# GroupNorm on one core: 16 instead of 12 chunks of each tile summed on TensorE, and SyncE's last wait moved from a branch to a semaphore increment

## The chip, the cores and the metric

The kernel runs on one core of a Trainium2 chip. The metric is the device time of one execution in microseconds (us). A kernel on one core has one number per execution.

Names: PE is TensorE, DVE is VectorE, ACT is ScalarE, POOL is GpSimd, SP is SyncE. A "q" behind a name (SPq) is that engine's queue of instructions that are not counted as work: waits, branches, DMA issues.

## The reference

```python
B, C, H, W = 128, 1024, 32, 16          # x is bfloat16; 32 groups of 32 channels
xr = x.reshape(B, 32, 32, H, W)
mu  = xr.mean(axis=(2, 3, 4), keepdims=True)
var = ((xr - mu) ** 2).mean(axis=(2, 3, 4), keepdims=True)
xn  = (xr - mu) / sqrt(var + 1e-5)
return xn.reshape(B, C, H, W) * g[None, :, None, None] + b[None, :, None, None]
```

Input and output are 134.2 MB each. A tile is 128 partitions (4 samples x 32 groups) of 16384 bfloat16 numbers, 4.19 MB; there are 32 tiles.

## The kernel before

Four engines work on a ring of six tiles in SBUF; POOL only makes constants at the start. For each tile:

- SP loads it, and later stores it from the same slot of the ring.
- The sum of each row is shared out. PE adds chunks of 512 columns into PSUM by multiplying them with an identity matrix. DVE adds the remaining columns pairwise in one instruction, whose accumulated result lands in PSUM beside PE's sums.
- ACT sums those 513 numbers to the mean, squares the tile around it in two halves, and makes the standard deviation.
- DVE makes scale and shift and normalises the tile in place with 32 instructions; it signals after each quarter.

The parts that matter, with cuts marked by `...`:

```python
SLOTS = 6                                   # ring of 6 tiles
RUNS = (2, 3, 3, 3, 3, 3, 3, 3, 3, 6)       # stores issued in a row, then the loads they free
NQ = 4
PE_CHUNKS = 12
MM_FREE = 512
PAIRED = F - PE_CHUNKS * MM_FREE            # columns paired on DVE; F = 16384

def on_sync(e):
    def load(j):
        if j >= SLOTS:
            e.wait_ge(st[j % SLOTS], 16 * (j // SLOTS))
        e.dma_start(out=slot(j), in_=x_v[j]).then_inc(ld[j % SLOTS], 16)
    def store(i):
        w = F // store_parts(i)             # the last tile goes in 4 parts, all others in 1
        for p in range(store_parts(i)):
            e.wait_ge(done, NQ * i + NQ // store_parts(i) * (p + 1))
            e.dma_start(out=..., in_=...).then_inc(...)
    ...
    e.wait_ge(s_fin, ...)                   # the last thing SP does

def one(c, t):                              # PE, per tile
    for k in range(PE_CHUNKS):
        if k == 0:                 e.wait_ge(ld[c], (t + 1) * 16)
        elif k == PE_CHUNKS - 2:   e.wait_ge(meaned[(c - 2) % SLOTS], t + 1)
        elif k == PE_CHUNKS - 1:   e.wait_ge(paired, t * SLOTS + (c + 1))
        mm = add_up(sums(c), slot(c)[:, k * MM_FREE : (k + 1) * MM_FREE], k)
    ...

def pair(i):                                # DVE, one tile ahead
    lo, n = PE_CHUNKS * MM_FREE, PAIRED // 2
    e.wait_ge(first_in, i + 1)
    e.scalar_tensor_tensor(out=jp[:], in0=part(i, lo, n), scalar=1.0, in1=part(i, lo + n, n),
        op0=ALU.mult, op1=ALU.add, accum_out=ps[...], saturate=False).then_inc(paired, 1)

with nc.Fori(0, NT, 1, engines=[e.engine]) as i:      # DVE's loop
    with e.If(i < NT - 1):
        e.drain()
        pair(i + 1)
    e.wait_ge(stded, i + 1)
    ...                                     # reciprocal, scale, shift: three short instructions
    for k, a in enumerate(parts):           # 32 normalising instructions
        ts = e.tensor_scalar(out=a, in0=a, scalar1=scl[:, k : k + 1], scalar2=bia[:, k : k + 1], ...)
        if (k + 1) % KQ == 0:
            ts.then_inc(done, 1)
```

## Time and profile before

| | before |
|---|---|
| median of 3 runs | 632.13 us (631.5 to 632.31) |
| span of the profiled run | 630.7 us |
| queue of loads and stores, share of 16 DMA engines | 99.1% |
| DVE busy | 529.6 us (84%) |
| ACT busy | 504.0 us (80%) |
| PE busy | 156.7 us (25%) |

First, lines of the profile's page of before. The first gives busy time and share of each engine; the rows under it cut the span into 40 equal slices: DMA is the busy share of the 16 DMA engines in tenths, GB/s what they moved. The last is the line of the queue with the loads and stores (packets, MB, share).

```profile
PE 156.7 (25%) x385; PEld 0.2 (0%) x2; DVE 529.6 (84%) x1185; ACT 504.0 (80%) x258; POOL 1.0 (0%) x8
...
DMA  8999999999999999999999999999999999999996
GB/s 366 432 432 409 434 436 432 432 434 434 428 432 432 432 434 430 434 430 432 432 432 428 432 432 432 432 432 432 432 432 432 432 426 432 430 430 436 432 421 271
...
q1 hardware_dynamic: 9648, 268.44, 99.1%
```

The GB/s row is flat, at 426 to 436 in nearly every slice, and the engines' rows are not. What sets the 432 GB/s, loads and stores together, is not shown. 268.4 MB at 432 GB/s are 621.4 us of the 630.7.

Second, the table by stretches for before: start and end, length, busy time and count of PE, PEld, DVE, ACT and POOL, the clock granted to PE, the DMA share, GB/s. The last two stretches are the end of the kernel.

```profile
75.00:200.00 125.00, 30.02 (x76) 0.00 (x0) 120.09 (x274) 114.28 (x58) 0.00 (x0) 0.60 1.01 434
200.00:400.00 200.00, 54.98 (x133) 0.00 (x0) 174.01 (x384) 164.96 (x85) 0.00 (x0) 0.59 1.00 432
400.00:540.00 140.00, 32.15 (x85) 0.00 (x0) 121.51 (x278) 115.66 (x59) 0.00 (x0) 0.59 1.00 432
613.00:620.00 7.00, 0.00 (x0) 0.00 (x0) 7.00 (x23) 0.00 (x0) 0.00 (x0) 0.50 0.89 375
624.00:629.00 5.00, 0.00 (x0) 0.00 (x0) 0.00 (x0) 0.00 (x0) 0.00 (x0) 0.50 0.23 98
```

Read the first row closely: from 75 to 200 us DVE is busy 120.09 of 125 us, 96%. The same row shows the DMA engines at a share of 1.01. (This view counts a packet, its time and its bytes, wholly in the stretch where it starts, so a share can come out a little over 1.)

Third, the timeline of before, only DVE's pairing instruction of four tiles: start, duration, engine, line, what it does, and in brackets how long DVE sat idle ahead of it and for whom.

```profile
203.16 5.49 DVE L254 SCALAR_TENSOR_TENSOR jp<-ring 128x5120 fp8e5 x1 [0.50 <-issue]
220.40 5.49 DVE L254 SCALAR_TENSOR_TENSOR jp<-ring 128x5120 fp8e5 x1 [0.50 <-issue]
237.63 5.49 DVE L254 SCALAR_TENSOR_TENSOR jp<-ring 128x5120 fp8e5 x1 [0.50 <-issue]
259.68 5.49 DVE L254 SCALAR_TENSOR_TENSOR jp<-ring 128x5120 fp8e5 x1 [5.30 <-PE ps L178]
```

Where a tile is already there, DVE needs 17.24 us from one pairing to the next. The DMA needs 8.39 MB (a load and a store) at 432 GB/s, 19.4 us. So every few tiles DVE runs out of tiles and waits, as at 259.68, for PE's first matmul of a tile, which itself waits for the load.

### The profile page before, as it was taken

Reading aid. Unit: us, or ns where it says so; the run is one execution under the profiler, and the core shown is the slowest. Engines: PE = TensorE matmul, PEld = TensorE weight load, DVE = VectorE, ACT = ScalarE, POOL = GpSimd, SP = SyncE. Lnnn points to the kernel's source line nnn. Section 1 sums busy time; section 2 is a strip of 40 time slices with the busy share of each in tenths; the row PEclk is TensorE's granted clock in tenths of the full one; section 3 lists DMA queues with packets and bytes.
Section 4 is the critical chain, followed back from the end, with each engine's and each line's share of the span. In section 5 each row is a group of like instructions: output and inputs, shape, how many; then the busy total and the mean of one; then the engine's idle time right before and its main releaser. Section 6 shows DMA issues by size and latency. Waiting matters only on the chain.

```text
span 630.7 us, 2595 instructions
## 1 busy us (share of the span) xinstructions
PE 156.7 (25%) x385; PEld 0.2 (0%) x2; DVE 529.6 (84%) x1185; ACT 504.0 (80%) x258; POOL 1.0 (0%) x8
## 2 busy tenths in 40 slices
PE   1433333212223220332053014202220430053000
PEld 0000000000000000000000000000000000000000
DVE  1669999999999999699789959995998699599963
ACT  0798999999999999689948977894999499859960
POOL 0000000000000000000000000000000000000000
PEclk9766655566665765666566557656665665565555
DMA  8999999999999999999999999999999999999996
GB/s 366 432 432 409 434 436 432 432 434 434 428 432 432 432 434 430 434 430 432 432 432 428 432 432 432 432 432 432 432 432 432 432 426 432 430 430 436 432 421 271
DMA packets 9745, 268.45 MB, mean 426 GB/s; under 512 B 1168, under 2 KB 1168, under 8 KB 1168
## 3 DMA queue, kind: packets, MB, share of 16 engines
q1 hardware_dynamic: 9648, 268.44, 99.1%
q10 hardware_dynamic: 96, 0.00, 0.0%
q14 instruction: 1, 0.01, 0.0%
HBM read 134.22 MB, written 134.22 MB: 426 GB/s over the span
## 4 chain that ended last, share of the span: by engine, by line
DMA 44%; ACT 40%; DVE 7%; issue 4%; PE 2%; DVEq 2%; SPq 0%
ACT ja L224 37%; DMA out_dram<-ring 28%; DMA ring<-in_x_dram 16%; DVE ring L287 6%; PE ps L178 2%; ACT jm L216 2%; DVEq L270 1%; ACT var L234 1%; ACT std L238 1%; DVE jp L254 1%; DVEq L273 0%; DVE bia L281 0%; DVE scl L277 0%; DVEq L275 0%; DVEq L254 0%
## 5 line engine op out<-in xcount | busy, mean ns | idle before, releaser
L224 ACT ACTIVATE ja<-ring,nm 128x8192 fp8e5<-128x8192 bf16 x64 | 455.8, 7122 | 2.1
L287 DVE TENSOR_SCALAR ring<-ring,scl,bia x1024 | 333.7, 413 | 1.2
L178 PE MATMUL ps<-ring,eye 128*128 128x512 bf16 x384 | 156.5, 581 | 424.9 <-DVE jp L254 292.5
L254 DVE SCALAR_TENSOR_TENSOR jp<-ring 128x5120 fp8e5 (+1 forms) x32 | 175.8, 5493 | 60.7 <-PE ps L178 48.7
L216 ACT ACTIVATE jm<-ps 128x513 fp8e5<-128x513 f32 x32 | 19.2, 602 | 98.7 <-PE ps L178 98.7
L275 DVE RECIPROCAL rstd<-std 128x1 f32 x32 | 6.3, 198 | 11.9 <-ACT std L238 11.9
L224 ACT ACTIVATION_READ_ACCUMULATOR ja<-ring,nm 128x1 f32 x64 | 11.9, 186 | 0.0
L281 DVE SCALAR_TENSOR_TENSOR bia<-scl,nm,gb 128x32 f32<-128x32 f32 x32 | 8.0, 251 | 4.2
L238 ACT ACTIVATE std<-sq,var 128x1 f32<-128x1 f32 x32 | 9.4, 294 | 1.0
L234 ACT ACTIVATE var<-sq,eps_t 128x1 f32<-128x1 f32 x32 | 9.4, 294 | 1.0
L266 DVE COPY gb<-gb_p 128x64 f32<-128x64 f32 x1 | 0.2, 225 | 11.5 <-PE gb_p L173 11.5
L277 DVE TENSOR_SCALAR scl<-gb,rstd 128x32 f32<-128x32 f32 x32 | 7.7, 241 | 1.1
L216 ACT ACTIVATION_READ_ACCUMULATOR jm<-ps 128x1 f32 x32 | 6.2, 194 | 0.0
L254 DVE DVE_READ_ACCUMULATOR jp<-ring (+1 forms) x32 | 4.5, 142 | 0.0
L173 PE MATMUL gb_p<-gb_b,rep 32*128 32x64 bf16 x1 | 0.2, 205 | 11.3 <-DMA gb_b<-in_b_dram 11.3
L212 ACT ACT_TABLE_LOAD x1 | 1.3, 1283 | 1.9 <-issue 1.9
L155 POOL TENSOR_SCALAR_AFFINE_SELECT rep<-ones_b 32x128 bf16<-32x128 bf16 x1 | 0.3, 303 | 0.0
L151 POOL TENSOR_SCALAR_AFFINE_SELECT eye<-ones_b 128x128 bf16<-128x128 bf16 x1 | 0.3, 293 | 0.4 <-issue 0.4
L212 ACT ACTIVATE warm<-eps_t 128x1 f32<-128x1 f32 x1 | 0.2, 203 | 0.0
L145 POOL MEMSET ones_b<- 128x128 bf16 x1 | 0.2, 205 | 0.5 <-SPq L294 0.5
L175 PEld LDWEIGHTS <-eye 128*128 128x128 bf16 x1 | 0.1, 105 | 0.1
L173 PEld LDWEIGHTS gb_p<-gb_b,rep 32*128 32x128 bf16 x1 | 0.1, 100 | 11.3 <-issue 11.3
(5 smaller groups left out, 0.5 us busy)
## 6 DMA issues: line engine op xcount, KB each, us to landing
ring<-in_x_dram SPq DMA_DIRECT2D x32, 4096.0 KB, 29.1
out_dram<-ring SPq DMA_DIRECT2D x31, 4096.0 KB, 31.3
out_dram<-ring SPq DMA_DIRECT2D x4, 1024.0 KB, 7.0
gb_b<-in_g_dram ACTq DMA_DIRECT2D x1, 2.0 KB, 6.5
gb_b<-in_b_dram ACTq DMA_DIRECT2D x1, 2.0 KB, 9.7
```

The costliest lines, as they stand in the source:

```text
L178: return e.add_instruction(mybir.InstMatmult(name=nc.get_next_instruction_name(), engine=e.engine, start_tensor_calc=(k == 0), stop_tensor ...
L212: e.activation(out=warm[:], in_=eps_t[:], func=ACT.Sqrt)
L216: e.activation(out=jm[:], in_=sums_and_pairs(c), func=ACT.Identity, scale=-inv_n, accum_out=nm[:, c : c + 1], saturate=False,).then_inc(me ...
L224: e.activation(out=ja[:], in_=slot(c)[:, h * (F // 2) : (h + 1) * (F // 2)], func=ACT.Square, bias=nm[:, c : c + 1], scale=1.0, accum_out= ...
L234: e.activation(out=var[:], in_=sq[:, 0:1], func=ACT.Identity, bias=eps_t[:], scale=inv_n).then_inc(varred[c], 1)
L238: e.activation(out=std[:, c : c + 1], in_=sq[:, 1:2], func=ACT.Sqrt, bias=var[:], scale=inv_n).then_inc(stded, 1)
L254: e.scalar_tensor_tensor(out=jp[:], in0=part(i, lo, n), scalar=1.0, in1=part(i, lo + n, n), op0=ALU.mult, op1=ALU.add, accum_out=ps[:, bas ...
L270: e.drain()
L275: e.reciprocal(out=rstd[:], in_=std[:, bass.ds(i % SLOTS, 1)]).then_inc(inverted, 1)
L277: e.tensor_scalar(out=scl[:], in0=gb[:, 0:KC], scalar1=rstd[:], scalar2=None, op0=ALU.mult).then_inc(scaled, 1)
L281: e.scalar_tensor_tensor(out=bia[:], in0=scl[:], scalar=nm[:, bass.ds(i % SLOTS, 1)], in1=gb[:, KC : 2 * KC], op0=ALU.mult, op1=ALU.add,). ...
L287: ts = e.tensor_scalar(out=a, in0=a, scalar1=scl[:, k : k + 1], scalar2=bia[:, k : k + 1], op0=ALU.mult, op1=ALU.add,)
```

## The change

The intent: take a fifth of the pairing off DVE, the busiest compute engine, and give it to PE, which is busy 25% of the time. And let SP end on an instruction of its own that carries the last wait; before, that wait sat on the branch that closes the section (in the trace of before, SP's compare-and-branch at 629.4 us, 33 ns long).

```diff
-PE_CHUNKS = 12
+PE_CHUNKS = 16
...
-    s_gb, s_ones, s_eye, s_gbp, s_fin = (
-        sem(n) for n in ("gbl", "ones", "eye", "gbp", "fin")
+    s_gb, s_ones, s_eye, s_gbp, s_fin, s_end = (
+        sem(n) for n in ("gbl", "ones", "eye", "gbp", "fin", "end")
...
-                e.wait_ge(st[j % SLOTS], 16 * (j // SLOTS))
+                e.wait_ge(
+                    st[j % SLOTS], 16 * sum(store_parts(i) for i in range(j % SLOTS, j, SLOTS))
+                )
...
         e.wait_ge(s_fin, 16 * sum(store_parts(i) for i in range(NT - SLOTS, NT)))
+        e.sem_inc(s_end, 1)
```

The third piece gives the same numbers as before, since only the last tile is stored in parts and no load waits for it.

## The prediction

> **What bounds it now.** The DMA engines. The page's slices show them at nine tenths or more in every slice but the first and last, at 426 to 436 GB/s. The queue table gives the load and store queue 99.1% of 16 engines' span. Stretches give 434 GB/s from 75 to 200 us and 432 from 200 to 540. The kernel moves 268.4 MB, and 268.4 MB at 432 GB/s is 621.4 us. The load of the first tile starts after about 2 us, and the last store, issued at 620.2, lands 9.1 us later; that leaves the 630.7 us span. [...] DVE (84% busy) and ACT (80%) are second limits: a tile costs the DMA 8.39 MB / 432 GB/s = 19.4 us, DVE 17.24 us (timeline, one pair instruction to the next where DVE never waits), ACT about 15.7 us.
>
> **What the change does.** PE adds 16 chunks of 512 instead of 12. Eleven matmuls in a row take 3.9 to 4.85 us, so about 0.4 us each: 4 more are about 1.7 us a tile, and PE busy rises from 157 to about 205 to 212 us. DVE's pairing instruction reads 4096 instead of 5120 pairs: 5.49 us becomes about 4.4 us (estimate, in proportion), 1.1 us less a tile, 35 us in all: DVE busy falls from 529.6 to about 494.5. DVE's cycle in an unstarved stretch falls from 17.24 to about 16.2 us, and ACT's wait of 1.4 us for the last matmul mostly closes. When a tile's load comes late (at 551.3 us in the waits), the last matmul now starts 6.57 us after the landing, because of the pairing. After, 15 chunks must precede it: about 15 x 0.43 = 6.5 us, so PE takes over and nothing is won there. The changed load wait has the same value. The semaphore increment on SyncE replaces a wait held by a branch: one event of 0.02 us after the last landing (existing ones took 17 to 21 ns).
>
> **On the critical path.** In the body nothing: DVE gets done earlier, stores queue earlier, and the DMA queue was already never empty. Only the tail can gain. The last two tiles are paced by DVE and ACT; they should end 1 to 2 us earlier (last normalising instruction at about 618.5 instead of 620.2). The DMA runs at only 375 GB/s from 613 to 620, so at most 0.9 us of starvation can be filled. [...] I expect 0 to 0.8 us.
>
> **Time.** 631.8 us, 8 in 10 between 630.2 and 633.4. Chances: faster by over 2% 0.01, within 2% 0.98, slower 0.01.
>
> **What the profile would show.** DMA slices still 432 GB/s, queue share about 99%; the pairing instruction at 4.4 us; 512 matmuls; DVE busy near 494; DVE idle up by some 35 us, ended by PE's first matmul.
>
> **What would make it wrong.** Earlier stores changing how reads and writes interleave, so that the rate of 432 moves; [...] PE's longer sum delaying the tiles enough to starve the stores, which would show as slices below 430 in mid-span.

The forecast's sum: the 632.13 us measured before, less 0 to 0.8 us won at the end, is 631.3 to 632.1, and 631.8 was put down.

## More of the kernel before

Executions of one kernel scatter by about 0.15% around their median (nine of before, in one set of runs: 631.70 to 632.75 us around 632.57), so differences of less than that need several rounds, and they are given with a 95% interval.

Last, the page's chain of waits that ended last, by engine, for before:

```profile
DMA 44%; ACT 40%; DVE 7%; issue 4%; PE 2%; DVEq 2%; SPq 0%
```

This line needs care. It reads as if ACT held 40% of the path. It follows, at every step, one releaser. Where two streams run side by side and each is sometimes the last one, it takes one of them.

## The result and the profile after

Ratios here and below are the mean time of one kernel's fast runs over that of the other's fast runs of the same rounds, so not quite the ratio of the medians quoted.

| | before | after |
|---|---|---|
| median | 632.22 us of 4 runs | 632.85 us of 4 runs (632.11 to 633.51) |
| ratio | | 1.0011, 95% interval 0.9994 to 1.0029 |
| PE busy | 156.7 us | 184.9 us |
| DVE busy | 529.6 us | 497.3 us |
| ACT busy | 504.0 us | 504.1 us |
| last store issued, landing after | 620.2, 9.1 us | 618.0, 11.9 us |

DVE lost 32.3 us of work and the time stayed where it was. The same lines of the page after:

```profile
PE 184.9 (29%) x508; PEld 0.2 (0%) x2; DVE 497.3 (79%) x1185; ACT 504.1 (80%) x258; POOL 1.0 (0%) x8
...
DMA  8999999999999999999999999999999999999995
GB/s 366 432 432 405 438 438 434 432 432 436 430 430 434 432 438 432 432 430 432 432 432 432 432 432 432 432 432 432 430 432 434 434 432 432 434 430 436 434 422 241
...
q1 hardware_dynamic: 9648, 268.44, 98.9%
```

The GB/s row is the same row, to within a few units in any slice but the last. The same stretches after:

```profile
75.00:200.00 125.00, 35.37 (x97) 0.00 (x0) 113.57 (x275) 119.33 (x62) 0.00 (x0) 0.62 1.00 433
200.00:400.00 200.00, 65.20 (x179) 0.00 (x0) 161.39 (x379) 158.79 (x84) 0.00 (x0) 0.64 1.00 433
400.00:540.00 140.00, 38.49 (x108) 0.00 (x0) 115.28 (x281) 116.25 (x58) 0.00 (x0) 0.62 1.00 432
613.00:620.00 7.00, 0.00 (x0) 0.00 (x0) 4.99 (x16) 0.00 (x0) 0.00 (x0) 0.50 0.93 393
624.00:629.00 5.00, 0.00 (x0) 0.00 (x0) 0.00 (x0) 0.00 (x0) 0.00 (x0) 0.50 0.11 48
```

And DVE's pairing in the timeline after:

```profile
200.58 4.43 DVE L257 SCALAR_TENSOR_TENSOR jp<-ring 128x4096 fp8e5 x1 [5.70 <-PE ps L181]
216.76 4.42 DVE L257 SCALAR_TENSOR_TENSOR jp<-ring 128x4096 fp8e5 x1 [0.50 <-issue]
233.30 4.42 DVE L257 SCALAR_TENSOR_TENSOR jp<-ring 128x4096 fp8e5 x1 [0.50 <-issue]
259.99 4.43 DVE L257 SCALAR_TENSOR_TENSOR jp<-ring 128x4096 fp8e5 x1 [10.81 <-PE ps L181]
```

These four lines against the four of before hold the case. Each pairing is 1.07 us shorter, and tiles that are there follow each other after 16.2 to 16.5 us instead of 17.24. But the tile that came at 259.68 before comes at 259.99 now. DVE just waits for it 10.81 us instead of 5.30. What is saved on DVE turns into waiting for the next load.

The mean lengths are 5493 ns for 5120 elements and 4426 ns for 4096: (5493 - 4426) / 1024 = 1.042 ns per element, and 158 ns beside it. This line, an estimate from the two lengths, gives 2.29 us for the 2048 elements of the run with 24 chunks below, and the trace there has 2.29. For the pieces of 1024 elements that are added further below, which have no accumulated output, it gives 1225 ns; the trace has 1226.

The chain of waits after:

```profile
DMA 53%; ACT 20%; DVE 15%; issue 5%; PE 3%; DVEq 2%; SPq 0%
```

ACT's share halved although ACT does exactly the same work in the same time. So the share of a compute engine in this chain was not a measure of how much time it costs.

### The profile page after: what moved, and what is told of

Read it like the earlier page. It is cut to its first block, busy times and chain, and to the rows that moved or that the text cites. A ratio compares the mean times of both kernels' runs of the same rounds, so it can differ in the third digit from the quotient of the medians.

```text
span 631.2 us, 2718 instructions
## 1 busy us (share of the span) xinstructions
PE 184.9 (29%) x508; PEld 0.2 (0%) x2; DVE 497.3 (79%) x1185; ACT 504.1 (80%) x258; POOL 1.0 (0%) x8
## 4 chain that ended last, share of the span: by engine, by line
DMA 53%; ACT 20%; DVE 15%; issue 5%; PE 3%; DVEq 2%; SPq 0%
DMA out_dram<-ring 33%; DMA ring<-in_x_dram 21%; ACT ja L227 18%; DVE ring L290 14%; PE ps L181 3%; ACT jm L219 1%; DVEq L273 1%; DVEq L276 1%; DVE jp L257 0%; ACT var L237 0%; ACT std L241 0%; DVE bia L284 0%; DVE scl L280 0%; DVEq L257 0%; DVE rstd L278 0%
## 5 line engine op out<-in xcount | busy, mean ns | idle before, releaser
L181 PE MATMUL ps<-ring,eye 128*128 128x512 bf16 x507 | 184.7, 536 | 394.6 <-DVE jp L257 218.2
L257 DVE SCALAR_TENSOR_TENSOR jp<-ring 128x4096 fp8e5 (+1 forms) x32 | 141.6, 4426 | 85.6 <-PE ps L181 74.1
```

Source lines behind the costliest of these rows:

```text
L181: return e.add_instruction(mybir.InstMatmult(name=nc.get_next_instruction_name(), engine=e.engine, start_tensor_calc=(k == 0), stop_tensor ...
```

## The experiments

The theory: in the body, the DMA rate is the limit. DVE and ACT have slack in every tile, so a change of DVE's work moves only waits. At the end, the landing of the last store is set by what is queued in the DMA engines, not by when the last store is issued. The rivals: (a) the shorter pairing did bring a gain, and PE's longer sum or SP's increment took it back; (b) the engines' waits for each other leave the DMA idle, so that it isn't the floor; (c) the end follows DVE. Every experiment was run with the kernel before on the same chip.

### Each half of the change alone

```diff
 # sem_only: the changed kernel with
-PE_CHUNKS = 16
+PE_CHUNKS = 12
 # k16_only: the kernel before with
-PE_CHUNKS = 12
+PE_CHUNKS = 16
```

> Only the SyncE part of the change (the increment after the last wait), with the 12 chunks of before. Theory: the increment costs about 0.02 us and nothing else moves: ratio to before 1.000, within 0.998 to 1.002. Rival, that the wait's new place costs (or saves) the 0.6 us by which the changed kernel's median lies higher: ratio 1.001 or the gap from the last store's landing to the end of the span grows from 1.4 us.

> Only the 16 chunks, with SyncE's wait as before. Theory: ratio 1.000, within 0.998 to 1.002; DVE busy 497 us, PE about 185 us; the last store is issued near 618 us and still lands near 629.5 us. Rival, that the pairing's saved time reaches the end: 2 us faster (ratio 0.997).

Measured: with the increment (and the rewritten wait of the loads) alone 632.22 us, ratio 0.9996 (0.9982 to 1.0010). With the 16 chunks alone 632.64 us, ratio 1.0003 (0.9989 to 1.0016). Both as the theory had it, and neither half hides a gain or a loss of the other. With 16 chunks alone the last store was issued at 617.6 us and landed 11.7 us later, at 629.3; with 12 chunks and the increment, it was issued at 620.1 and landed 9.1 us later, at 629.2. From the last landing to the end of the span it is 1.39 us before and with the 16 chunks alone, and 1.29 us after and with the increment alone. So the increment costs nothing there; if anything the end comes 0.1 us sooner, far too little to show in the time. It does have a use: its wait is an instruction of its own in the profile. Of SP's waits after, this line has the engine and line, whom it waited for, total, count and longest:

```profile
SPq L145 <- DMA out_dram<-ring: 11.6, 1, 11.6
```

Before, the wait sat on a branch, and the list of waits has no line for it.

### The changed kernel again

No edit.

> The changed kernel once more, unaltered, because its median lay 0.1% over that of before while neither half of the change did. Theory: that was the scatter of the runs: ratio between 0.998 and 1.002 with an interval that holds 1. Rival, that both halves together cost something that neither costs alone: 1.001 again with an interval above 1.

Measured: 632.51 us, before 632.64, ratio 0.9995 (0.9981 to 1.0008). The 0.1% was scatter.

### Only the DMA

All compute is taken out, and with it what makes the stores wait: a store now waits for the load of its tile. The output is x, wrong.

```diff
-                e.wait_ge(done, NQ * i + NQ // store_parts(i) * (p + 1))
+                e.wait_ge(ld[i % SLOTS], 16 * (i // SLOTS + 1))
...
-        on_gpsimd(nc.gpsimd)
-        on_tensor(nc.tensor)
-        on_scalar(nc.scalar)
-        on_vector(nc.vector)
```

> Only SyncE's loads and stores, with the stores waiting for the tile's load instead of for DVE; no compute (the output is x, wrong on purpose). Theory: all 268.4 MB at 432 GB/s plus start and end, 626 to 632 us: the floor lies within 1% of both kernels. Rival, that waits for compute leave the DMA engines idle for a good part: under 615 us.

Measured: 630.54 us, before 632.49, ratio 0.9975 (0.9959 to 0.9992). Its GB/s row, and its stretches in the table (no engine but POOL appears in it):

```profile
GB/s 367 434 434 419 434 431 431 434 431 434 434 434 434 429 434 434 434 423 434 434 434 431 434 431 434 434 434 434 431 434 434 434 427 434 434 434 431 434 434 283
```

```profile
75.00:200.00 125.00, 0.00 (x0) 1.00 1.00 433
200.00:400.00 200.00, 0.00 (x0) 1.00 1.00 432
613.00:620.00 7.00, 0.00 (x0) 1.00 0.93 392
624.00:629.00 5.00, 0.00 (x0) 1.00 0.10 44
```

This settles rival (b). Moving the bytes alone, in these transfers and this order, takes all but a quarter of a per cent of the time. Everything that the engines compute is worth at most about that. It also shows that the low rates of the last stretches are no lack of stores: here SP began to issue the last store at 571.9 us, and it landed 55.9 us later, so all stores were queued for the whole of the end, and the rates from 613 to 620 and from 624 to 629 are still 392 and 44 GB/s.

The 375 and 392 GB/s from 613 to 620 us are themselves mostly a matter of counting, since a packet's bytes are put where it starts. With each packet's bytes spread evenly over its own time (worked out from the packet records of the traces), before moves 418 to 428 GB/s in every microsecond from 613 to 624 us, and this run 427 to 430 from 613 to 623. Over the seven microseconds up to 620 the two differ by 22 kB, 0.05 us at 432 GB/s. The rate really falls only after 623 us.

### DVE with far less work

The changed kernel, but of the 32 normalising instructions of a tile only the first two of each quarter are run. The result is wrong.

```diff
             for k, a in enumerate(parts):
+                if k % KQ > 1:
+                    continue
                 ts = e.tensor_scalar(...)
-                if (k + 1) % KQ == 0:
+                if k % KQ == 1:
```

> The changed kernel with 8 of 32 normalising instructions a tile (wrong result on purpose): DVE loses another 7.8 us a tile, 250 us in all. Theory: still the DMA, 629 to 633 us; the last store is issued about 8 us earlier (near 610 us) and still lands near 629 us. Rival, that the end follows DVE: 6 to 8 us faster, near 624 us.

Measured: 631.61 us, ratio to before 0.9987 (0.9971 to 1.0004). DVE's busy time fell to 249.8 us, less than half of before, and the time did not move. The last store was issued at 607.7 us. The start and length of the last issue, in this run and in the one with only the DMA (most issues take 0.33 to 0.43 us, these took longer, so the start has to be read and not reckoned back from the end):

```profile
607.65 1.03 SPq L131 DMA_DIRECT2D out_dram<-ring  x1
```

```profile
571.89 1.41 SPq L131 DMA_DIRECT2D out_dram<-ring  x1
```

In the list of DMA issues, the line of the last store has what was moved, the queue, count, size and the time from issue to landing. Four kernels, in the order before, after, this one, and only the DMA:

```profile
out_dram<-ring SPq DMA_DIRECT2D x1, 1024.0 KB, 9.1
```

```profile
out_dram<-ring SPq DMA_DIRECT2D x1, 1024.0 KB, 11.9
```

```profile
out_dram<-ring SPq DMA_DIRECT2D x1, 1024.0 KB, 20.8
```

```profile
out_dram<-ring SPq DMA_DIRECT2D x1, 1024.0 KB, 55.9
```

The same megabyte took 9.1 to 55.9 us, because what is measured is mostly the queue ahead of it. Add the issue: 620.2 + 9.1 = 629.3, 618.0 + 11.9 = 629.9, 607.7 + 20.8 = 628.5, 571.9 + 55.9 = 627.8. The store was issued up to 48 us earlier and all four landed within 2.2 us. Rival (c) falls: an issue 12.6 us earlier than before, with less work on DVE, brought the landing forward by 0.9 us in the one execution profiled, and nothing that the times can tell from noise.

### PE with a longer sum

```diff
-PE_CHUNKS = 16
+PE_CHUNKS = 24
```

> 24 chunks on PE, 8 paired on DVE. A late tile's sum now waits some 10 us for PE instead of 6, DVE's pairing falls to 2.2 us. Theory: nothing at the end, 631 to 634 us, slices still 432 GB/s, DVE busy near 427 us. Rival, that PE's longer sum delays the stores: DMA slices below 425 GB/s in mid-span and over 636 us.

Measured: 632.22 us, ratio 0.9999 (0.9982 to 1.0016); DVE busy 429.7 us, PE 227.8, and 432 GB/s from 200 to 400 us. So PE could take twice as many chunks as before without a price, and without a gain.

### The change where the DMA is not the limit

From the seventh tile on, only half of each tile is loaded; the rest of the slot keeps what was there. The result is wrong. 213.9 MB remain, 495 us at 432 GB/s. Once with 12 chunks, once with 16, both with the increment.

```diff
-            e.dma_start(out=slot(j), in_=x_v[j]).then_inc(ld[j % SLOTS], 16)
+            w = F if j < SLOTS else F // 2
+            e.dma_start(out=slot(j)[:, 0:w], in_=x_v[j][:, 0:w]).then_inc(ld[j % SLOTS], 16)
```

> From the seventh tile on, only half of each tile is loaded (the result is wrong on purpose); 12 chunks. 213.9 MB are left, 495 us at 432 GB/s. Theory: the DMA stops being the limit and DVE's cycle of 17.24 us a tile takes over: 37 + 31 x 17.24 + 10.4 + 8.4 = 590 us, between 583 and 600. Rival, that DVE's stretches are not a limit of their own and the tile's latency or the queue's order decides: nearer to 500, or above 610.

> The same half loads with 16 chunks. Theory: the 1.1 us that the shorter pairing saves on DVE now shows in every tile: a cycle of 16.2 to 16.5 us, 36.5 + 31 x 16.4 + 10.4 + 8.4 = 564 us, between 558 and 572, that is 4 to 5% less than the same kernel with 12 chunks. Rival, that PE's longer sum gives the gain back: within 1% of it.

Measured: 588.37 us with 12 chunks and 564.35 us with 16, 24.0 us or 4.1% less. The timelines, pairing instructions only, first 12, then 16 chunks:

```profile
202.85 5.49 DVE L258 SCALAR_TENSOR_TENSOR jp<-ring 128x5120 fp8e5 x1 [0.50 <-issue]
220.09 5.49 DVE L258 SCALAR_TENSOR_TENSOR jp<-ring 128x5120 fp8e5 x1 [0.50 <-issue]
```

```profile
211.72 4.42 DVE L258 SCALAR_TENSOR_TENSOR jp<-ring 128x4096 fp8e5 x1 [0.50 <-issue]
227.89 4.42 DVE L258 SCALAR_TENSOR_TENSOR jp<-ring 128x4096 fp8e5 x1 [0.50 <-issue]
244.64 4.43 DVE L258 SCALAR_TENSOR_TENSOR jp<-ring 128x4096 fp8e5 x1 [0.50 <-issue]
```

With fewer bytes, DVE waits for no load from the third tile on: only 0.50 us stand ahead of each pairing, in which the profile shows no wait. A tile costs 17.24 us with 12 chunks. With 16, tiles of 16.2 and 16.75 us take turns, 16.5 on average. So of the 1.07 us by which the pairing got shorter, about 0.8 us a tile arrive: 24.0 us over 31 tiles. The rest goes to ACT, not to PE. In every second tile DVE now waits 0.47 us for ACT's standard deviation, as in the first line below. PE, on the other hand, waits for DVE's pairing in 30 tiles (second line: total, count, longest), 323.3 us in all:

```profile
232.86 0.16 DVE L279 RECIPROCAL rstd<-std 128x1 f32 x1 [0.47 <-ACT std L242]
```

```profile
PE ps L182 <- DVE jp L258: 323.3, 30, 12.6
```

So rival (a) falls as well: PE's longer sum takes nothing back. The change does what it is for; this kernel just has no place for it.

### How much work DVE can take

Idle pairing work is added to DVE ahead of the real pairing: two instructions of 1024 elements (2.3 us a tile in DVE's busy time), then four. The result stays right. A first form, which wrote to the tile that the real pairing writes, was a race. So the added work writes a small tile of its own, in small pieces.

```diff
             e.wait_ge(first_in, i + 1)
+            for again in range(2):          # dve_plus4: range(4)
+                if again:
+                    e.drain()
+                e.scalar_tensor_tensor(out=jq[:], in0=part(i, lo, n // 4), scalar=1.0,
+                    in1=part(i, lo + n, n // 4), op0=ALU.mult, op1=ALU.add, saturate=False)
```

> The changed kernel with about 2.3 us of idle pairing work added to DVE in each tile (result right): DVE's cycle grows to 18.5 us, still under the 19.4 us that a tile costs the DMA. Theory: the body hides it; only the end moves, as the last tiles end some 4 to 5 us later: 633 to 640 us, 10 times less than the 74 us added. Rival, DVE bound: over 690 us.

> The changed kernel with about 4.6 us of idle pairing work added to DVE in each tile (result right), twice the dose of the last run, whose cycle was 18.46 us. Theory: DVE's cycle becomes 20.8 us, over the 19.4 us of the DMA, and DVE takes over: 36.5 + 31 x 20.8 + 10.4 + about 9 = 700 us, between 690 and 706. Rival, that the first dose's 4 us was a cost per added microsecond and not a threshold: twice that, 640 us.

Measured: 636.35 us with the first dose, ratio 1.0064 (1.0047 to 1.0081), and 707.20 us with the second, ratio 1.1177 (1.1160 to 1.1194). The first dose added 74 us of DVE work and cost some 4 us; the second added as much again and cost 71 us more. That is a threshold, not a price per microsecond. In the timeline of the first dose the pairings follow each other after 18.46 us, under the 19.4 us of the DMA. With the second dose they do so after 21.06:

```profile
204.14 4.42 DVE L265 SCALAR_TENSOR_TENSOR jp<-ring 128x4096 fp8e5 x1
225.20 4.42 DVE L265 SCALAR_TENSOR_TENSOR jp<-ring 128x4096 fp8e5 x1
246.26 4.42 DVE L265 SCALAR_TENSOR_TENSOR jp<-ring 128x4096 fp8e5 x1
```

And its GB/s row is flat no more, since here the DMA waits for compute (398 GB/s from 200 to 400 us):

```profile
GB/s 377 425 441 418 360 416 386 149 416 416 431 334 424 416 357 414 420 414 357 416 405 368 388 444 416 357 398 405 446 312 431 420 353 416 427 424 308 191 165 357
```

Two expectations were missed in part. The second dose came out 1.2 us above its range: its four pieces took 5.13 us a tile in the timeline, where 4.6 were expected. For the first dose the total was right, but its place was not: not only the end moved. This stretch of it shows the DMA at half its rate:

```profile
120.00:125.00 5.00, 0.00 (x0) 0.00 (x0) 4.58 (x11) 4.97 (x2) 0.00 (x0) 0.65 0.52 216
```

At that time SP had issued three stores from 85.7 us on, the last at 122.7 us, when DVE had finished that tile. The loads that stand behind it in SP's order came only at 123.0. So a cycle shorter than the DMA's is not enough early on. As we read it, DVE first has to catch up with the six tiles loaded ahead, and with a margin of only 1 us a tile that takes so long that the queue ran dry here; no run was made to test this reading. At the end, the last store was now issued at 627.7 us and landed 5.5 us later. That is the other side of the threshold: when DVE comes later than the queue, the landing follows DVE.

## Why the prediction was right

- **What bounds the kernel: right.** The DMA alone takes 630.54 us, before takes 632.5 and after the same. The slices hold 432 GB/s in both.
- **What the change does on DVE: right.** A pairing was predicted at 4.4 us and took 4.43. DVE busy was predicted at 494.5 us and is 497.3. The cycle was predicted at 16.2 us and is 16.2 to 16.5 in the lines shown; over the eight cycles from 47.5 to 179.2 us, where DVE waits for no load, 16.2 and 16.75 take turns and the mean is 16.5. That ACT would be waited for in every second tile was not foreseen. DVE's idle time rose by 32.8 us (span less busy time: 101.1 before, 133.9 after). Of that, the waits for PE's first matmul account for 25.4 us (48.7 to 74.1 in the list of waits).
- **What it adds on PE: right in kind, too large in size.** The prediction put PE busy at 205 to 212 us, with 0.4 us for each added matmul; it is 184.9. The added 4 matmuls a tile were costed close to what they took in before at a granted clock of 0.50 (11 in a row in 4.85 us from 551.3 us on). The granted clock rose from a mean of 0.598 to 0.639; at 1.00, nine matmuls took 1.98 us after (from 555 us on). In the stretch from 550 to 560 us, before ran its 12 matmuls at 0.50 throughout; after had a mean of 0.77 there, with 1.00 from 555 us on, in the middle of its 16. After, the first matmul started at 551.9 and the clock was full about 3 us later; but before, the 4.85 us of matmuls in a row left it at 0.50 up to 560 us. How long the work lasts does not alone say when the clock rises here. (Five of the 512 matmuls are missing from the records after.)
- **PE takes over where a tile comes late: wrong for one tile that was named, and without effect.** Predicted was that the last matmul would start about 6.5 us after the landing at 551 us, as before. It started 5.50 us after it (551.89 to 557.39), and still waited for DVE, because PE's clock had risen. For the tile that came at 317.6 us PE did set the pace: all its 16 matmuls, 6.03 us, stand in the chain of waits. From the landing of a late tile to the start of ACT's mean it is 5.95 to 6.4 us after and 7.0 to 7.2 before (the six such tiles from 258 us on), so something was won there, which the prediction ruled out. The run with 24 chunks shows that this latency buys and costs nothing here.
- **The end: the mechanism right, one term not.** The last normalising instructions were predicted to end at about 618.5 us and did so at 618.0. The prediction allowed up to 0.9 us from filling a starvation between 613 and 620 us. With all stores long queued, the same view still shows 392 GB/s there, and with the packets' bytes spread over their time the gap shrinks to 0.05 us: next to nothing was starved. The last store of these runs lands within 2.2 us of the same moment however early it is issued, until DVE comes later than the queue. That the total fell into the predicted range says little by itself: a gain of 0 to 0.8 us, 0.13% at most, lies inside the scatter of the runs, and the intervals neither show nor exclude it.
- **SP's increment: right.** It takes 0.017 us, and there is nothing in the time.
- **The risk named first, another interleaving of reads and writes: did not occur** in any run that kept the DMA queue full. Even the run with no compute, where stores queue 50 us deep, moves 432 GB/s.

Why the rate falls off before the last store has landed, though that store is long queued (44 GB/s from 624 to 629 us in the run with no compute, whose last store landed at 627.8), stays open. The records do not say which engine a packet ran on. No run that moves all the bytes was faster by more than the one with no compute, and that lies only a quarter of a per cent under before.

## What to carry to other kernels

When the row of transfer rates is flat at one value from end to end, take the compute out, run the transfers alone, and compare: if that takes the same time, cutting compute will not help, however busy an engine looks. Here a cut on an engine that is 96% busy in a stretch was worth nothing, because its time for a tile lay below the DMA's; compare the two, 17.24 us against 19.4 us here, before trusting a busy share or a chain of waits. Mind the margin too: at 18.46 us the kernel already lost 4 us. A store's time from issue to landing was mostly queue here: add it to the issue time, and see whether the landing moves.
